# Two pads that move the weights and one input tile of a fused attention and MoE kernel by 128 and 288 bytes

## The chip, the cores and the metric

The kernel runs on one core of a Trainium2 chip. The metric is the device time of one execution in microseconds (us), the median over several executions. Lower is better.

## What is computed

Attention with mixed heads (a 12 by 12 matrix before the softmax, another after it), whose output is the input of a bilinear MoE block without gates:

```python
batch, n_heads, seq, head_dim = (4, 12, 448, 64)
n_tokens, d_model, d_ff = (1792, 768, 1536)

def _attn_ref(q, k, v, w_pre, w_post):
    scores = scale * np.matmul(q, k.transpose(0, 1, 3, 2))
    scores = np.einsum('bhij,hg->bgij', scores, w_pre)
    attn = softmax(scores)                      # max, exp, sum, divide
    attn = np.einsum('bhij,hg->bgij', attn, w_post)
    return np.matmul(attn, v).astype(np.float32)

def _moe_ref(x, w_a, w_b, w_out):               # x: the attention output, 1792 x 768
    a = x @ w_a
    b = x @ w_b
    return (a * b @ w_out).astype(np.float32)
```

## The kernel before

One program runs on all five engines, in an order that is written out by hand. It has two stages.

The attention stage takes 92 steps of up to 20 queries each: scores (`qk`, L241), head mixing (`premix`, L305), softmax (`smax`), a second mixing (`postmix`, L348) and the product with v (`av`, L384). Its output goes to DRAM, per batch b, as `xd[b]`.

The MoE stage works on four blocks of 448 tokens (b = 0 to 3). It first goes over f = 0 to 11 (128 columns of d_ff each) and b: `run_a` and `run_b` each make one 128x448 result in PSUM, from 6 slices of the contraction of 768. Then the output part goes over b and m (6 blocks of 128 output rows): `run_o` makes one 128x448 result from 12 slices of the contraction of 1536. Every product is taken in three matmuls, since both operands are split into a high and a low part: `mm3` (L545 to L547) multiplies high by high, high by low and low by high. So `run_a` and `run_b` are 18 matmuls each, `run_o` is 36, and the MoE has 12 x 4 x 36 + 24 x 36 = 2592 of them, all of one shape: 128x128 weights (the stationary operand: `wh` and `wl`) and 448 moving columns (`xhl` in the first part, `hh` and `hl` in the output part), 4 bytes per element. Each matmul has its own weight load. TensorE loads the weights of the next matmul while the present one runs.

The tiles lie in SBUF where the pools put them, one pool behind the other. What matters here is the byte address in a partition at which a tile begins, modulo 256. A moving slice has 448 x 4 = 1,792 = 7 x 256 bytes and a weight slice 128 x 4 = 512 = 2 x 256 bytes, so all slices of a tile have the tile's own value:

| tile | begins at byte | modulo 256 |
|---|---|---|
| x of b = 0, b = 1, b = 3 | 39,040; 17,536; 60,544 | 128 |
| x of b = 2 (pool `mx`) | 200,288 | 96 |
| all h (`hh`, `hl`) | 17,536; 39,040; 60,544; 83,584 | 128 |
| all weights (pool `mw`: `wh`, `wl`) | 175,712; 181,856; 188,000; 194,144 | 96 |

The text calls **lead** the address of the weights less that of the moving operand, modulo 256. It is 96 - 128 = 224 for b = 0, 1 and 3 and for all of the output part, and 0 for b = 2.

The pool `mc` holds the four buffers in which weights are converted. The pools of k, q and one tile of the scores (`short`) come behind it, and are closed when the MoE's pools `mw` and `mx` take their place (`open_moe`). x of b = 0, 1 and 3 and h stand in the pool `big`, in buffers of the attention stage, ahead of `mc`.

Of the kernel before, what the change touches and what calls it, by code (L numbers as in the profile page):

```python
# [7 lines left out]
F32 = mybir.dt.float32  # L8
# [13 lines left out]
def talking_heads_bilinear_kernel(  # L22
# [39 lines left out]
    OWN = 3  # L62
    SPREAD = 2
    RAW_AT = (73, 77)
    scale = 1.0 / float(D) ** 0.5

    chunks = []
# [26 lines left out]
    x_p = ctx.enter_context(tc.tile_pool(name="x", bufs=2))  # L94
    ps = ctx.enter_context(tc.tile_pool(name="ps", bufs=2, space=PSUM))
    mc = ctx.enter_context(tc.tile_pool(name="mc", bufs=1))
    short = ExitStack()
    k_p = short.enter_context(tc.tile_pool(name="k", bufs=10))
    q_p = short.enter_context(tc.tile_pool(name="q", bufs=4))
# [349 lines left out]
    mo, xt, wt, raws = {}, {}, {}, {}  # L449

    def open_moe():
        short.close()
        mo["w"] = ctx.enter_context(tc.tile_pool(name="mw", bufs=2))
        mo["x"] = ctx.enter_context(tc.tile_pool(name="mx", bufs=1))

    def load_x(b, parts=range(KD)):
        if b not in xt:
            pool, tag = ((big, "s"), (big, "s"), (mo.get("x"), "x"), (big, "pt"))[b]
            xt[b] = pool.tile([128, 2, KD, S], F32R, tag=tag, name="xhl")
        for i in parts:  # L460
            nc.sync.dma_start(out=xt[b].bitcast(F32)[:, 1, i], in_=xd[b][:, i])
# [14 lines left out]
    def load_raw(u, parts=1):  # L476
        kind, i, e = u
        t = raw_space().bitcast(I32).rearrange("p (c t) -> p c t", t=2)
        to, src = t.rearrange("p (k f) t -> p k (f t)", k=KD), (w_ab if kind == "f" else w_out)[i, e].bitcast(I32)
        n = KD // parts  # L480
        raws[u] = t
        return [
            lambda k=k: nc.sync.dma_start(out=to[:, k:k + n], in_=src[:, k:k + n]) for k in range(0, KD, n)
        ]
# [129 lines left out]
    def plan_moe():  # L614
# [5 lines left out]
        def load(n, fns):  # L620
            for i, fn in enumerate(fns):
                todo_at.setdefault(n + i, []).append(fn)
# [10 lines left out]

        todo_at.setdefault(RAW_AT[0], []).append(lambda: load(RAW_AT[0] + 1, load_raw(order[0], 3)))
        todo_at.setdefault(RAW_AT[1], []).append(lambda: load(RAW_AT[1] + 1, load_raw(order[1], 3)))
        s0 = last_prep + 1
# [16 lines left out]
    with tc.manual_schedule():  # L653
# [37 lines left out]
        for s in range(NU + 2):  # L691
            now[0] = s
            if s == last_prep + 1:
                open_moe()
# [164 lines left out]
```

## Time and profile before

| | |
|---|---|
| median of 3 runs | 918.71 us (914.97 to 920.8) |
| the profiled execution | 918.93 us |
| its span, from the first to the last instruction | 917.2 us |
| TensorE (PE) busy | 885.6 us (97%) |
| VectorE (DVE), ScalarE (ACT), GpSimd (POOL) busy | 515.8, 376.2, 440.2 us |

A row of the profile names a line of the program, an engine, an operation and its tiles. PE is TensorE's matmuls, PEld its weight loads, which run beside them. The duration shown for a matmul is longer than its share of the engine, since consecutive matmuls overlap: what a matmul costs is the time from its start to the start of the next one, called the **pitch** here. The view in order of time gives starts to 0.01 us, so a pitch is best read over many matmuls: the distance of two starts by the number of matmuls between them.

### The profile page before, as it was taken

The page shows a single profiled execution, that of the slowest core. Times are in us where ns is not written, and L with a number is a line of the kernel's source. Part 1 is how long each engine was busy: PE and PEld are TensorE (multiplying, and loading weights), DVE is VectorE, ACT ScalarE, POOL GpSimd, SP SyncE. Part 2 cuts the span into 40 slices and gives each one's busy share as a digit, 9 for nine tenths or more (in the row PEclk, how much of TensorE's full clock was granted, in tenths as well). Part 3 has the DMA queues.
Part 4 walks back from the last instruction along what each step waited for, and adds up shares of the span by engine and source line. Part 5 has one row for each costly group of instructions (what it writes and reads, how often), then busy time and mean ns, then how long its engine had stood idle before and what let it go on. Part 6 is the DMA issues. An engine that isn't in the chain of part 4 may idle for free.

```text
span 917.2 us, 27078 instructions
## 1 busy us (share of the span) xinstructions
PE 885.6 (97%) x11440; PEld 704.7 (77%) x11440; DVE 515.8 (56%) x907; ACT 376.2 (41%) x848; POOL 440.2 (48%) x547
## 2 busy tenths in 40 slices
PE   8899999999999898899999999999999999999998
PEld 4456565565656555799999999999999989999997
DVE  5667776576766676667654575556653545151500
ACT  5667677577666565421111111111111334343421
POOL 4687777576767663124423342324322255455552
PEclk9999999999999999999999999999999999999999
DMA  5798777568656775714533333334331664646441
GB/s 163 190 220 187 191 199 190 134 184 209 171 155 184 194 188 146 244 66 143 173 116 116 116 134 120 127 121 142 133 118 48 237 253 134 254 134 258 141 139 57
DMA packets 81850, 147.45 MB, mean 161 GB/s; under 512 B 41758, under 2 KB 61322, under 8 KB 80706
## 3 DMA queue, kind: packets, MB, share of 16 engines
q1 hardware_dynamic: 53602, 108.05, 36.7%
q0 software_dynamic: 28128, 37.68, 16.1%
q8 instruction: 90, 1.47, 0.7%
q14 instruction: 30, 0.25, 0.1%
HBM read 80.23 MB, written 26.74 MB: 117 GB/s over the span
## 4 chain that ended last, share of the span: by engine, by line
PE 89%; DMA 2%; issue 2%; DVE 2%; SPq 2%; ACT 1%; POOL 1%; ACTq 0%; DVEq 0%; POOLq 0%
PE xp L384 9%; PE pp L348 9%; PE pst L241 7%; PE mp L305 7%; PE pa L545 6%; PE pa L546 6%; PE pa L547 6%; PE po L546 6%; PE po L547 6%; PE po L545 6%; PE pb L545 6%; PE pb L546 6%; PE pb L547 6%; DMA sb<-s 2%; SPq L285 1%
## 5 line engine op out<-in xcount | busy, mean ns | idle before, releaser
L285 POOL DMA_DIRECT2D sb<-s x350 | 201.3, 584 | 93.9 <-PE mp L305 52.2
L504 POOL TENSOR_TENSOR cvm<-cvm,cvr 128x768 int32<-128x768 int32 x36 | 66.3, 1843 | 205.5 <-DVE cvm L503 205.5
L535 POOL TENSOR_TENSOR wl<-v,wh 128x768 fp32r<-128x768 f32 x48 | 93.6, 1974 | 106.7 <-ACT wh L534 106.7
L315 DVE TENSOR_REDUCE nm<-mp 124x1 f32<-124x448 f32 x180 | 104.4, 619 | 67.2 <-PE mp L305 66.8
L318 ACT ACTIVATE a<-mp,nm 124x448 f32<-124x448 f32 x180 | 112.6, 630 | 60.7 <-DVE nm L315 60.7
L384 PEld LDWEIGHTS xp<-pt,v 120*64 120x64 f32 x1536 | 76.9, 140 | 68.6 <-issue 48.0
L557 ACT COPY sa<-pa 128x448 f32<-128x448 f32 x48 | 25.6, 533 | 241.3 <-PE pa L547 241.3
L348 PE MATMUL pp<-kr,a 60*56 60x60 f32 x5760 | 103.4, 216 | 10.3 <-issue 9.4
L363 ACT COPY pt<-pp 120x480 f32<-120x480 f32 x176 | 91.1, 574 | 49.7 <-PE pp L348 49.6
L348 PEld LDWEIGHTS pp<-kr,a 60*56 60x56 f32 x5760 | 89.1, 127 | 28.4 <-issue 15.8
L567 DVE TENSOR_TENSOR hf<-pb,sa 128x448 f32<-128x448 f32 x47 | 29.4, 625 | 144.4 <-PE pb L547 107.0
L305 PE MATMUL mp<-sb,wp 60*64 60x448 f32 x720 | 100.7, 550 | 7.3 <-DMA sb<-s 3.4
L546 PE MATMUL po<-hl,wh 128*128 128x448 f32 x288 | 106.4, 369 | 0.5 <-DVE hl L582 0.5
L545 PE MATMUL po<-hh,wh 128*128 128x448 f32 x288 | 106.3, 369 | 0.0
L547 PE MATMUL po<-hh,wl 128*128 128x448 f32 x288 | 106.3, 369 | 0.0
L545 PE MATMUL pa<-xhl,wh 128*128 128x448 f32 x288 | 105.9, 368 | 0.0
L547 PE MATMUL pa<-xhl,wl 128*128 128x448 f32 x288 | 105.9, 368 | 0.0
L546 PE MATMUL pa<-xhl,wh 128*128 128x448 f32 x288 | 105.9, 368 | 0.0
L545 PE MATMUL pb<-xhl,wh 128*128 128x448 f32 x282 | 103.8, 368 | 0.0
L546 PE MATMUL pb<-xhl,wh 128*128 128x448 f32 x282 | 103.8, 368 | 0.0
L547 PE MATMUL pb<-xhl,wl 128*128 128x448 f32 x282 | 103.8, 368 | 0.0
L582 DVE TENSOR_TENSOR hl<-hl,hh 128x448 fp32r<-128x448 f32 x48 | 57.6, 1254 | 79.6 <-ACT hh L581 79.6
(75 smaller groups left out, 1375.0 us busy)
## 6 DMA issues: line engine op xcount, KB each, us to landing
sb<-s POOLq DMA_DIRECT2D x346, 105.0 KB, 4.6
v<-wod SPq DMA_DIRECT2D x24, 768.0 KB
v<-in_w_ab_dram SPq DMA_DIRECT2D x22, 768.0 KB
hd<-hf SPq DMA_DIRECT2D x48, 224.0 KB
v<-in_w_out_dram SPq DMA_DIRECT2D x12, 768.0 KB
k<-in_k_dram SPq DMA_DIRECT2D x24, 224.0 KB
v<-in_v_dram SPq DMA_DIRECT2D x48, 112.0 KB
xhl<-xd SPq DMA_DIRECT2D x24, 224.0 KB
```

What stands on the lines that cost most here:

```text
L285: (nc.sync if u <= AH and i % 2 else nc.gpsimd).dma_start(out=sbt[u][i % 2][r:r + m * H], in_=rows)
L305: nc.tensor.matmul(mt[u, i // 2][col:col + M], lhsT=wp[r:r + m, :M], rhs=tiles[i % 2][r:r + m])
L315: nc.vector.tensor_reduce(nm[:m], mp[:m], axis=AXX, op=ALU.max, negate=True)
L318: nc.scalar.activation(a[:m], mp[:m], ACTF.Exp, bias=nm[:m], scale=1.0, accum_out=rss[u][:m, j:j + 1])
L348: nc.tensor.matmul(pp_t[i][64 * e:64 * e + C, H * r:H * r + H, j, :m], lhsT=a[rows, keys:keys + C], rhs=kr[rows, j, :, :m],)
L363: nc.scalar.copy(to[:C2, :, o + QB * i:o + QB * i + QB], pp_t[i][:C2].rearrange("p x j t -> p x (j t)"))
L384: nc.tensor.matmul(xp[64 * e:64 * e + 64, p % 3, :n], lhsT=vt[b % 2][g][:C2, h % G, r], rhs=ptt[a][:C2, r, h, :n], start=(r == 0), stop=(r ...
L504: lambda: nc.gpsimd.tensor_tensor(m, m, r, op=ALU.add),
L535: nc.gpsimd.tensor_tensor(ll[:, sl], raw, hh.bitcast(F32)[:, sl], op=ALU.subtract)
L545: nc.tensor.matmul(o, lhsT=hh[:, k0 + kk], rhs=mh[:, kk], start=(kk == 0), stop=False)
L546: nc.tensor.matmul(o, lhsT=hh[:, k0 + kk], rhs=ml[:, kk], start=False, stop=False)
L547: nc.tensor.matmul(o, lhsT=ll[:, k0 + kk], rhs=mh[:, kk], start=False, stop=(kk == n - 1))
```

## The change

Two tiles that nothing reads or writes are added. The first, of 32 x 4 = 128 bytes in a partition, is in the pool `mc`, so that everything behind it begins 128 bytes later. The second, of 40 x 4 = 160 bytes, stands ahead of the x of b = 2 in the pool `mx`, which so begins 288 bytes later.

```diff
@@ -62,6 +62,8 @@
     RAW_AT = (73, 77)
+    PAD_W = 32
+    PAD_X = 40
@@ -94,6 +96,7 @@
     mc = ctx.enter_context(tc.tile_pool(name="mc", bufs=1))
+    mc.tile([128, PAD_W], F32, tag="pad", name="pad")
     short = ExitStack()
@@ -452,6 +455,7 @@
         mo["x"] = ctx.enter_context(tc.tile_pool(name="mx", bufs=1))
+        mo["x"].tile([128, PAD_X], F32, tag="pad", name="pad")
```

| tile | begins at byte, after | modulo 256 |
|---|---|---|
| x of b = 0, 1, 3 and all h | as before | 128 |
| x of b = 2 | 200,576 | 128 |
| all weights | 175,840; 181,984; 188,128; 194,272 | 224 |
| conversion buffers `cvm`, `cvr` | 128 bytes later | 224, before 96 |
| k, q, the third tile of the scores | 128 bytes later | each by 128 |

The lead is 224 - 128 = 96 everywhere. Every engine has the same instructions in the same order, with the same waits, in both kernels; only addresses differ. In the attention stage k and q move together, and both operands of L305, L348 and L384 stay where they were.

## Rows read from the trace of the kernel before

**Rows 1.** The page: engines' busy time, and granted clock by slice of the span.

```profile
PE 885.6 (97%) x11440; PEld 704.7 (77%) x11440; DVE 515.8 (56%) x907; ACT 376.2 (41%) x848; POOL 440.2 (48%) x547
PEclk9999999999999999999999999999999999999999
```

**Rows 2.** The page: the chain that ended last, by engine.

```profile
PE 89%; DMA 2%; issue 2%; DVE 2%; SPq 2%; ACT 1%; POOL 1%; ACTq 0%; DVEq 0%; POOLq 0%
```

**Rows 3.** By stretch: engines' busy us (instructions), clock, DMA share, GB/s.

```profile
0.00:379.10 379.10, 351.69 (x8849) 217.60 (x8849) 254.55 (x588) 252.93 (x598) 241.33 (x443) 0.98 0.71 183
379.10:734.00 354.90, 354.90 (x1730) 324.90 (x1729) 207.03 (x276) 56.56 (x96) 109.23 (x58) 1.00 0.38 132
734.00:913.40 179.40, 178.88 (x865) 162.18 (x863) 54.20 (x43) 66.02 (x151) 89.64 (x46) 1.00 0.50 174
```

**Rows 4.** In order of time (start us, duration us): f=0, b=0 and 1.

```profile
382.80 0.36 PE L545 MATMUL pst<-xhl,wh 128*128 128x448 f32 x1
...
393.60 0.37 PE L545 MATMUL pa<-xhl,wh 128*128 128x448 f32 x1
```

**Rows 5.** In order of time: f=1, first matmuls of b=0, 2 and 3.

```profile
408.34 0.37 PE L545 MATMUL pa<-xhl,wh 128*128 128x448 f32 x1
...
423.22 0.36 PE L545 MATMUL pa<-xhl,wh 128*128 128x448 f32 x1
...
430.52 0.36 PE L545 MATMUL pa<-xhl,wh 128*128 128x448 f32 x1
```

**Rows 6.** In order of time: two first matmuls and the last of the output part.

```profile
742.24 0.37 PE L545 MATMUL po<-hh,wh 128*128 128x448 f32 x1
...
909.64 0.37 PE L545 MATMUL po<-hh,wh 128*128 128x448 f32 x1
...
913.15 0.37 PE L547 MATMUL po<-hh,wl 128*128 128x448 f32 x1
```

**Rows 7.** By line, 383.3:393.5: xcount | busy us, mean ns | idle.

```profile
L546 PE MATMUL pb<-xhl,wh 128*128 128x448 f32 x6 | 2.2, 362 | 0.0
```

**Rows 8.** By line, 423.4:430.4, b=2.

```profile
L546 PE MATMUL pb<-xhl,wh 128*128 128x448 f32 x6 | 2.2, 365 | 0.0
```

**Rows 9.** By line, 431.4:452.6, b=3, 0 and 1: matmuls and weight loads.

```profile
L546 PE MATMUL pb<-xhl,wh 128*128 128x448 f32 x18 | 6.6, 369 | 0.0
...
L546 PEld LDWEIGHTS pb<-xhl,wh 128*128 128x128 f32 x18 | 3.4, 188 | 0.3
```

**Rows 10.** By line, 383.3:393.5: weight loads.

```profile
L547 PEld LDWEIGHTS pb<-xhl,wl 128*128 128x128 f32 x6 | 1.1, 188 | 0.1
```

**Rows 11.** Warm-up matmuls at full clock: in order of time, and by line.

```profile
15.63 1.51 PE L145 MATMUL warm<-ones 128*128 128x128 f16 x24
...
L145 PE MATMUL warm<-ones 128*128 128x128 f16 x24 | 1.5, 220 | 0.0
```

**Rows 12.** Waits, 379 to 917.2 (waiter <- releaser: us in total, times, longest).

```profile
ACT sa L557 <- PE pa L547: 241.3, 48, 8.3
POOL cvm L504 <- DVE cvm L503: 203.5, 34, 16.5
ACT so L593 <- PE po L547: 113.2, 24, 6.8
DVE hf L567 <- PE pb L547: 107.0, 34, 6.8
PEld po L546 <- DVE hl L582: 0.9, 1, 0.9
PE po L546 <- DVE hl L582: 0.5, 1, 0.5
```

**Rows 13.** The chain that ended last, around the output part's start.

```profile
731.49 2.34 ACT hh L581 x5
734.81 5.01 DVE hl L582 x3
```

## The prediction

> **What bounds the kernel now.** I read the page's first two parts, the chain, then the stretches, and last single matmuls. TensorE is busy for 885.6 of 917.2 us at nine tenths or more of the full clock of 2.4 GHz in all slices [rows 1], and holds 89% of the chain that ended last [rows 2]. The chip thus waits for TensorE alone. Up to 379.1 us it works on attention, whose matmuls keep the distance between their operands' addresses. From 379.1 to 734.0 and from 734.0 to 913.4 us it does the 1728 and 864 matmuls of the MoE and is busy for all of 354.9 and for 178.88 of 179.4 us at clock 1.00 [rows 3]. In this stage every other engine waits for TensorE: ScalarE 241.3 us for `pa` and 113.2 us for `po`, VectorE 107.0 us for `pb`; GpSimd waits for VectorE (203.5 us), and TensorE itself once, 0.5 us [rows 12]. So the MoE's time is 2592 times the pitch, and all that can change it is the pitch.
>
> **The pitch is not one number**, though shape, clock and line are the same. From the first matmul of the second group (b=0, f=0) to the first of b=2 are 54 matmuls in 393.60 - 382.80 = 10.80 us: 200.0 ns each, at lead 224 [rows 4]. In f=1, b=2 takes 36 matmuls in 430.52 - 423.22 = 7.30 us, 202.8 ns at lead 0, and b=0 and b=1 take 72 in 423.22 - 408.34 = 14.88 us, 206.7 ns at lead 224 [rows 5]. The output part runs 45 groups of 18 from 742.24 to 909.64 us: 167.40 / 810 = 206.7 ns, lead 224 [rows 6]. b=2 repeats its 202.8 and the others their 206.7 in each of the f that follow. The matmuls' own durations follow: 362, 365 and 369 ns [rows 7, 8, 9], while the weight load takes 188 ns at either end of the scale [rows 9, 10]. What stretches is the stream of the 448 columns, not the load beside it.
>
> How much there is to take: the last 24 warm-up matmuls of 128 columns, with weight loads too, take 1.51 us, the last of them 220 ns [rows 11], so their pitch is (1510 - 220) / 23 = 56.1 ns. 128 columns at 2.4 GHz are 53.3 ns, which leaves 2.8 ns of fixed cost; 448 columns would be 186.7 + 2.8 = 189.5 ns. The MoE's matmuls stand 10.5, 13.3 and 17.2 ns above that.
>
> The sum of now: 72 matmuls (f=0, b=0 and 1) at 200.0, 12 x 36 = 432 of b=2 at 202.8, and the other 2088 at 206.7 (exactly 14.88/72) make 14.4 + 87.6 + 431.5 = 533.5 us. The trace has 913.15 - 379.09 = 534.1 us from first to last start, the 0.5 us wait among it, so the sum closes.
>
> **The change part by part.** It adds no instruction, wait or DMA; only addresses differ. Three edits:
>
> *Weights 128 bytes later.* The lead of b=0, 1, 3 and of the output part, 2160 matmuls, goes from 224 to 96. No row of before has lead 96, so its pitch has to be bounded. Below stands 189.5 ns, from a stream that shows no stretch. Above, the worst row is 206.7 ns; since nothing says that it is the worst there is, I go one step further. The two levels seen at lead 224, 200.0 and 206.7, lie 6.7 ns apart (16 clocks of 2.4 GHz); the next such step is 213.3 ns. Between these ends I take 200.0 ns. Leads 224 and 0 are neighbours on the circle of 256 bytes, 32 apart, and both are stretched; 96 lies 96 and 128 bytes away, in a part of the circle that the trace has not seen. If the stretch comes from the two streams meeting at the same place of a pattern of 256 bytes, it should be less there; if the pattern is 128 bytes or shorter, 96 and 224 are the same place, which the trace shows at 200.0 as well as at 206.7. 200.0 is the lower row, and lies near the middle of the floor and the common level.
>
> *x of b=2 to lead 96.* Its 432 matmuls leave 202.8 ns for whatever lead 96 gives. At 200.0 this is 1.2 us of gain, at 206.7 a loss of 1.7 us.
>
> *All else that moves* (conversion buffers, k, q, one tile of scores) I cost at nothing. k and q keep their distance, L305, L348 and L384 keep both operands. The conversions are on VectorE, ScalarE and GpSimd, which are busy for 207, 57 and 109 of 355 us in the first part and 54, 66 and 90 of 179 us in the second [rows 3]; the cover is TensorE's 533 us of matmuls, and would hold at the floor of 491 us too. DMA engines are at 0.38 and 0.50 there. One place has no cover: at the start of the output part TensorE waits 0.5 us for `hl` of VectorE [rows 12], which works from 734.81 on through 5.01 us of the chain, after ScalarE's `hh` [rows 13]. VectorE's pace there doesn't change, while the two blocks of matmuls ahead of it (72) end 72 x 6.7 ns = 0.5 us sooner at 200.0; I add 0.4 us to this wait.
>
> Sum: 2592 x 200.0 = 518.4 us in place of 533.5, -15.1 us, +0.4 us. Against the profiled execution, 918.93 us (0.2 above the median of the runs, so nothing is corrected): 904.2 us, 1.6% faster.
>
> A rule of the Trainium skill speaks against this. Its page "TensorE: Matmul & The Clock Gate" (section "Step-by-step: what each phase is for") has two independent SBUF read ports in TensorE, one for moving columns and one for weights, and says that loading the next weights takes no read bandwidth from the running matmul. By that rule the lead could not matter, and the sum would be nothing. The trace disagrees: pitch and duration differ by the tile that is read, 202.8 against 206.7 ns and 365 against 369 [rows 5, 8, 9].
>
> **Rivals.**
>
> *The streams no longer meet*: 189.5 ns everywhere. For it: both known leads are close together, and 96 is far from them. Against: even the best stretch seen is 10.5 ns above the floor, and the weight load sweeps 512 bytes, twice round the circle, so it may always meet the columns somewhere. 2592 x 189.5 = 491.2 us, -42.3: 876.6 us, with the wait of `hl` 877 to 878.
>
> *The change doesn't do what it says*: the pitch hangs on lead modulo 128 or less, or on where x itself begins. Then all settles at 206.7, since 2088 of the 2160 matmuls at lead 224 do so now, and b=2 loses its advantage: 2592 x 206.7 = 535.7 us, +2.2: 921.1 us. For it: 96 and 224 are alike modulo 128, and lead 224 has two levels with nothing but their history between them. If lead 0's 202.8 held everywhere instead, 525.7 us, -7.8: 911 us.
>
> *Lead 96 is worse*: one more step, 213.3 ns in all: 552.9 us, +19.4: 938.3 us. For it: the two leads seen do not show the worst. Against: they stand where small shifts of timing carry the pitch between levels, which looks like an edge rather than a quiet region. It decides from (533.5 + 9.2) / 2592 = 209.4 ns on.
>
> **How the numbers follow.** About 200.0 ns 0.33; at or near the floor (up to 195 ns) 0.20; 202.8 everywhere 0.07; all at 206.7 0.22; worse 0.18. The likeliest is 904.2 us, its own range 900 to 908. About 1% (9.2 us) is what a measurement here can tell from no change. Faster takes the first two cases, 0.53; same those at 202.8 and 206.7, 0.29; slower 0.18. The range leaves out the last: from 875 us, just below the floor's case, to 922 us, just above the case of no effect.
>
> **What would show it.** In the profile after, the MoE's stretch is 2592 pitches: 518 us if I am right, 491 at the floor, 536 without effect, 553 if worse. The mean durations of L545 to L547 should be 362 ns in all groups, b=2 as the others; 352 (362 - 10.5) would be the floor, 369 no effect, over 372 the last rival. Weight loads should stay at 188 ns, and the attention stage at 379 us. The wait of L546 for `hl` should stay under 2 us. The forecast is wrong if the groups of one lead still differ, if b=2 now differs from the others at the same lead, or if the stretch moves while the durations of matmuls don't.

## The result: 0.8% faster in the first set of runs, 13 us in four later ones, and a profile that hit the forecast

In 22 runs of each kernel the median went from 921.31 to 915.11 us; the ratio is 0.9919, with a 95% interval of 0.9892 to 0.9946. This is faster by 0.8%, half the forecast; the medians lie 6.2 us apart, where 14.7 were forecast. Seven executions of the changed kernel, all over 917.5 us, count as slow and are left out of the ratio; with six of them in (the seventh, 1415.06 us, had a granted clock of 0.556) the gain would be 0.6%. The profiled execution of the changed kernel took 903.93 us, the fastest of its 22, where the forecast was 904.2. Both are true, and the experiments are about how.

The page after, engines and chain, as [rows 1, 2]:

```profile
PE 868.3 (96%) x11440; PEld 703.2 (78%) x11440; DVE 518.8 (57%) x907; ACT 377.5 (42%) x848; POOL 442.5 (49%) x547
PE 76%; POOL 8%; issue 6%; DMA 5%; DVE 2%; ACT 1%; SPq 1%; POOLq 0%; ACTq 0%; DVEq 0%
```

By stretch, as [rows 3] (attention, first part of the MoE, output part; the columns are the same):

```profile
0.00:378.90 378.90, 349.37 (x8849) 216.74 (x8849) 255.14 (x588) 254.03 (x598) 242.81 (x443) 0.99 0.71 183
378.90:724.60 345.70, 345.70 (x1731) 324.53 (x1730) 209.63 (x276) 56.70 (x96) 110.29 (x58) 1.00 0.39 135
724.60:898.50 173.90, 173.23 (x865) 161.89 (x863) 53.98 (x43) 66.13 (x151) 89.39 (x46) 1.00 0.51 179
```

The attention stage is as long as before, though TensorE holds less of the chain: 76% of the whole against 89%. The first part went from 354.9 to 345.7 us, the output part from 179.4 to 173.9: 14.7 us, all of it in TensorE's own stream. In order of time, f=1, the first matmuls of b=0, 2 and 3, as [rows 5]:

```profile
407.79 0.36 PE L549 MATMUL pa<-xhl,wh 128*128 128x448 f32 x1
...
422.19 0.36 PE L549 MATMUL pa<-xhl,wh 128*128 128x448 f32 x1
...
429.39 0.36 PE L549 MATMUL pa<-xhl,wh 128*128 128x448 f32 x1
```

72 matmuls in 14.40 us and 36 in 7.20: 200.0 ns for b=0, 1 and 2 alike. The groups by line over 395 to 735 us, and the output part (740 to 895 us), as [rows 7 to 9], and the wait for `hl`, as [rows 12]:

```profile
L550 PE MATMUL pb<-xhl,wh 128*128 128x448 f32 x276 | 100.0, 362 | 0.0
L550 PE MATMUL po<-hl,wh 128*128 128x448 f32 x259 | 93.9, 362 | 0.0
PE po L550 <- DVE hl L586: 0.7, 1, 0.7
```

362 ns in all groups, which is the row that the forecast named. In this execution the whole MoE runs at 200.0 ns, but for its first matmul and the wait for `hl`.

### The profile page after: what moved, and what is told of

The parts are those of the page before. It is cut to its first block, busy times and chain, and to the rows that moved or that the text cites. A ratio compares the mean times of both kernels' runs of the same rounds, so it can differ in the third digit from the quotient of the medians.

```text
span 902.2 us, 27078 instructions
## 1 busy us (share of the span) xinstructions
PE 868.3 (96%) x11440; PEld 703.2 (78%) x11440; DVE 518.8 (57%) x907; ACT 377.5 (42%) x848; POOL 442.5 (49%) x547
## 4 chain that ended last, share of the span: by engine, by line
PE 76%; POOL 8%; issue 6%; DMA 5%; DVE 2%; ACT 1%; SPq 1%; POOLq 0%; ACTq 0%; DVEq 0%
POOL sb L288 6%; PE pa L549 6%; PE pa L550 6%; PE pa L551 6%; PE po L550 6%; PE po L551 6%; PE po L549 6%; PE pb L550 6%; PE pb L549 6%; PE pb L551 6%; PE xp L387 6%; PE pp L351 5%; PE mp L308 4%; PE pst L244 4%; DMA sb<-s 2%
## 5 line engine op out<-in xcount | busy, mean ns | idle before, releaser
L351 PE MATMUL pp<-kr,a 60*56 60x60 f32 x5760 | 104.6, 216 | 13.4 <-issue 12.8
L550 PE MATMUL po<-hl,wh 128*128 128x448 f32 x288 | 104.5, 363 | 0.7 <-DVE hl L586 0.7
L549 PE MATMUL pa<-xhl,wh 128*128 128x448 f32 x288 | 104.5, 363 | 0.0
L550 PE MATMUL pa<-xhl,wh 128*128 128x448 f32 x288 | 104.4, 362 | 0.0
L551 PE MATMUL po<-hh,wl 128*128 128x448 f32 x288 | 104.4, 362 | 0.0
L549 PE MATMUL po<-hh,wh 128*128 128x448 f32 x288 | 104.4, 362 | 0.0
L549 PE MATMUL pb<-xhl,wh 128*128 128x448 f32 x282 | 102.2, 362 | 0.0
L550 PE MATMUL pb<-xhl,wh 128*128 128x448 f32 x282 | 102.2, 362 | 0.0
```

The costliest lines, as they stand in the source:

```text
L351: nc.tensor.matmul(pp_t[i][64 * e:64 * e + C, H * r:H * r + H, j, :m], lhsT=a[rows, keys:keys + C], rhs=kr[rows, j, :, :m],)
L549: nc.tensor.matmul(o, lhsT=hh[:, k0 + kk], rhs=mh[:, kk], start=(kk == 0), stop=False)
L550: nc.tensor.matmul(o, lhsT=hh[:, k0 + kk], rhs=ml[:, kk], start=False, stop=False)
L551: nc.tensor.matmul(o, lhsT=ll[:, k0 + kk], rhs=mh[:, kk], start=False, stop=(kk == n - 1))
```

## The experiments

Theory A: the lead sets the pitch, and executions differ only in the attention stage. Theory B: a lead has several **levels** of the pitch; the stream of matmuls falls to one at its start or after a disturbance (called a **draw** here), and keeps it.

**The changed kernel, unaltered, profiled again** (four calls, each on another chip).

> The changed kernel, unaltered, profiled once more. The recorded profile of it has the MoE at 200.0 ns per matmul throughout (518.4 us), and its execution of 903.93 us is the fastest of 22, whose median is 915.1; the kernel before has a median of 921.3. Theory A (the lead fixes the pitch; the spread comes from the attention stage, up to 379 us): the MoE again takes 518 to 520 us with every matmul at 200.0 ns, and what exceeds 904 us lies before the first MoE matmul. Theory B (lead 96 has two levels as well, and which one holds is a matter of timing): part of the MoE runs at 203 to 207 ns, the MoE takes 522 to 536 us, and the attention stage ends at 379 us as before.

> The changed kernel, unaltered, in more rounds beside lead 192. Theory B gives its executions four places, by the level drawn at the MoE's entry (1728 matmuls) and after the wait for hl (the last 830 or so): 904 us (200.0 and 200.0), 910 (the output part at 206.7), 915 to 916 (the first part at 206.7), 921 (both), each with the 3 us or so that the attention stage varies by. If none but the lead counted, all would be at 902 to 909 us.

> The changed kernel, unaltered, once more in five rounds. Theory B: the profiled execution has the first part and the output part each at 200.0 or at 206.7 ns; in the five profiles so far both were at 200.0. Executions at 904 to 906 us plus 0, 5.5, 11.5 or 17 us, plus what this chip's attention stage takes beyond 379 us (on one chip it was 386 us). If only the attention stage varied, the profile again shows 519 us for the MoE and the excess ahead of it.

> The changed kernel, unaltered, beside lead 192 on one chip. In six profiles so far its MoE took 519.3 us and the attention stage 379 to 386 us; the executions that other calls timed lie at 903 to 912 us for the most part, those of the first set at 904 to 920. If the first set's longer executions came from second-level draws, this set should show steps of 5.5 and 11.5 us above its shortest that lead 192 lacks. If they came from the attention stage, both kernels spread alike.

Medians, beside the kernel before on the same chip: 905.05 against 917.86, 910.04 against 923.00, 909.61 against 923.43, 910.24 against 923.20 us; ratios 0.9880 (0.9843 to 0.9917), 0.9844 (0.9797 to 0.9891), 0.9880 (0.9829 to 0.9932), 0.9872 (0.9835 to 0.9910). The difference of the medians is 12.8 to 13.8 us in each. The profiles say where the rest went. By stretch (length, then PE busy, clock, DMA share, GB/s), the second repeat:

```profile
0.00:386.42 386.42, 354.08 (x8849) 0.98 0.70 179
386.42:732.13 345.71, 345.71 (x1730) 1.00 0.39 135
732.13:905.68 173.55, 172.88 (x865) 1.00 0.51 180
```

and the fourth, with two starts of its output part, 834 matmuls apart, and a group of that part (740 to 895 us):

```profile
0.00:381.50 381.50, 350.22 (x8848) 0.98 0.70 182
381.50:727.22 345.72, 345.72 (x1731) 1.00 0.38 135
727.22:906.31 179.09, 178.42 (x864) 1.00 0.49 174
...
733.55 0.36 PE L549 MATMUL po<-hh,wh 128*128 128x448 f32 x1
...
905.90 0.37 PE L549 MATMUL po<-hh,wh 128*128 128x448 f32 x1
...
L550 PE MATMUL po<-hl,wh 128*128 128x448 f32 x251 | 92.2, 367 | 0.0
```

Both theories get something. In the second repeat the attention stage is 7.5 us longer and the MoE is not. The first and the third are alike, with attention stages of 380.0 and 383.2 us. But in the fourth, 912.08 us, nothing was altered and the output part took 179.1 in place of 173.6 us: it fell to 206.7 ns (172.35 us / 834) after the wait for `hl`, at lead 96. Theory A is wrong. The matmuls there last 367 ns; at lead 224 they last 369 at the same pitch, so a duration tells the level only within a lead.

**A nudge of 56 ns at the entry.** One or two 16-bit matmuls of 128 columns ahead of the MoE's first matmul (in `run_a`; `range(2)` in the second kernel); no address of the MoE's operands changes:

```diff
         pa = ps.tile([128, 512], F32, tag="m", name="pa", bufs=3)[:, :S]
+        if f == b == 0:
+            for _ in range(1):
+                nc.tensor.matmul(pa[:, :128], lhsT=ones, rhs=ones)
         mm3(pa, hh, ll, x[:, 0], x[:, 1], KD)
```

> The changed kernel with one 16-bit matmul of 128 columns (56 ns) ahead of the first matmul of the MoE, which only moves its time against whatever the level is drawn from; all leads stay at 96. Theory B: the first part falls to 200.0 or to 206.7 ns and stays there for its 1728 matmuls (MoE 519 or 531 us). Theory A: 200.0 ns, 519 us.

> The same with two such matmuls. Theory B: 200.0 or 206.7 ns throughout the first part, not necessarily as with one. Theory A: 200.0 ns.

By stretch, the MoE's two parts with one nudge, then with two:

```profile
387.02:744.21 357.19, 357.19 (x1732) 1.00 0.38 131
744.21:923.32 179.11, 178.59 (x864) 1.00 0.50 174
```

```profile
389.11:734.81 345.70, 345.70 (x1731) 1.00 0.39 136
734.81:913.90 179.09, 178.42 (x864) 1.00 0.50 174
```

With one, all 2592 matmuls run at 206.7 ns and the MoE takes 536.3 us; that is the second rival's MoE, reached without a change of lead. With two, the first part is at 200.0 and the output part at 206.7. So the levels of lead 96 are worth 357.2 - 345.7 = 11.5 us and 179.1 - 173.6 = 5.5 us, drawn twice in an execution. Each of the two kernels ran once. That the nudge made the draw at the entry, and not chance, is likely, since the seven profiles of this MoE without it all entered at 200.0 ns; it is not shown.

**Each part of the change alone.** First only x of b=2 is moved, so that the lead is 224 throughout (`PAD_W` left out, `PAD_X = 8`); then only the weights (`PAD_X` left out), so that b=2 is at lead 0.

> One part alone: x of b=2 is moved by 32 bytes, the weights stay, so that the lead is 224 in the whole MoE. In the kernel before, lead 224 ran at 200.0 ns in f=0 (b=0, b=1) and at 206.7 ns ever after the first passage of b=2 at lead 0; the bursts at lead 224 gave 200.0, 204.4 and 206.7 ns. Theory A (the lead alone sets the pitch, and 224 is a 206.7 lead): 206.7 ns in all of the MoE, 535.7 us, 920 to 921 us. Theory B (each lead has several levels, and the stream keeps the one that it fell into until something disturbs it): with no b=2 at another lead to disturb it, the first part stays at the level at which f=0 enters; if that is 200.0 ns, the first part takes 346 us in place of 355, and the wait for hl at the start of the output part draws again: 906 us if it draws 200.0, 912 if 206.7.

> The other part alone: the weights 128 bytes later, x of b=2 left behind them, so that b=2 is at lead 0 and all else at lead 96. b=2 (432 matmuls) should run at 202.7 or 206.7 ns. Each passage of b=2 is a disturbance: if lead 96 returned to 200.0 by itself, the MoE would take 521 us; if it keeps what it falls into, b=3, 0 and 1 run at 200.0 or 206.7 in each f, 521 to 533 us.

By stretch, x alone, then the weights alone:

```profile
377.48:734.69 357.21, 357.21 (x1731) 1.00 0.38 131
734.69:913.83 179.14, 178.61 (x865) 1.00 0.50 174
```

```profile
380.37:727.60 347.23, 347.23 (x1730) 1.00 0.38 135
727.60:906.71 179.11, 178.44 (x864) 1.00 0.49 174
```

With x alone the profiled execution (919.59 us) entered at 206.7 and stayed there; three others, not profiled, took 905.87, 912.67 and 916.24 us, which would fit such draws. The ratio of these three is 0.9889 (0.9833 to 0.9945). With the weights alone b=2 runs at 202.7 and b=3 comes back to 200.0 in each f, so the first part loses 1.5 us; here the output part drew 206.7. Ratio 0.9940 (0.9898 to 0.9982).

**All leads.** Bursts of the same matmul behind the end of the kernel, the columns' start shifted by 32 bytes at a time. Two kernels have 36 bursts of 24; the third has 127, and in it (`SEQ` lists lead, length, columns of weights and moving columns of each burst):

```diff
+        def burst(hh, x, lead, n_, wc=128, cols=S):
+            mv, ws = x.rearrange("p f s -> p (f s)"), hh.rearrange("p k f -> p (k f)")
+            i = (96 - lead) // 32 % 8
+            t = ps.tile([128, 512], F32, tag="x", name="scan", bufs=1)[:wc, :cols]
+            for n in range(n_):
+                wo, mo_ = 128 * (n % 4), S * (n % 4) + 8 * i
+                nc.tensor.matmul(t, lhsT=ws[:, wo:wo + wc], rhs=mv[:, mo_:mo_ + cols], start=(n == 0), stop=(n == n_ - 1))
...
             run_o(j)
+        for lead, n_, wc, cols in SEQ:
+            burst(last, ht[B - 1][0], lead, n_, wc, cols)
```

> The changed kernel with 36 bursts of 24 matmuls of the same shape behind its end (128x128 weights, 448 columns, results unused), whose moving operand starts 0 to 7 times 32 bytes later, so that each lead of the circle of 256 bytes is visited, once from bursts at lead 96 and once from bursts at lead 0; four bursts move weights and columns together by 32, 64 and 160 bytes. It adds about 175 us. If the pitch is set by the lead modulo 256: lead 0 near 202.8 ns, 224 near 206.7 or 200.0, 96 at 200.0, and the others a curve between 189.5 and 213 ns; moving both operands together changes nothing. If the pattern has 128 bytes or less: leads 32 and 160, 64 and 192, 96 and 224 give the same. If it hangs on where the columns themselves begin: the bursts that move both change their pitch. The MoE ahead of the scan is another sample of the changed kernel: 200.0 ns by theory A, a mixture by theory B.

> The kernel before with the same 36 bursts behind its end, at the same sequence of leads (its weights lie 128 bytes elsewhere). The pitch of each lead should be that of the other scan if the lead alone counts, and differ by burst if the absolute addresses count. The MoE ahead of it is another sample of the kernel before: 206.7 ns at b=0, 1, 3 and in the output part and 202.8 at b=2, if its recorded profile is typical.

> The changed kernel with 127 bursts behind its end: 16 matmuls at leads 96, 192, 224 and 0, each entered from bursts of 12 and of 13 matmuls at each of the seven other leads (14 entries a lead), then bursts of 24 whose weights have 128, 64 and 32 columns, then bursts with 448, 320 and 224 moving columns. Theory B: the entries at 224 and 0 split between several levels, those at 96 and 192 fall nearly all to 200.0; theory A: one level per lead. If the stretch above 189.5 ns comes from the weight load's reading beside the columns, it shrinks with the weights' columns (10.5 ns at 128, about half at 64, about a quarter at 32) and stays, in ns per matmul, as the moving columns get fewer (320 columns 146.7 + 10.5 = about 147 ns at least with fixed cost, 224 about 107); if it is a fixed cost of such a matmul, it stays at 10.5 ns for fewer weights' columns.

The two scans agree in each burst to within 0.2 ns, though their absolute addresses differ. They are two executions, so in these bursts the level follows from the stream just before and is not chance. Moving weights and columns together left lead 96 at 200.0 ns; at lead 224 it gave 204.4 and 206.7, levels that this lead has unmoved too. Two bursts at lead 96 in the scan of the changed kernel, two starts of each, 15 matmuls apart:

```profile
924.67 0.56 PE L826 MATMUL scan<-hh,wh 128*128 128x448 f32 x2
...
927.67 0.56 PE L826 MATMUL scan<-hh,wh 128*128 128x448 f32 x2
...
935.01 0.57 PE L826 MATMUL scan<-hh,wh 128*128 128x448 f32 x2
...
938.11 0.56 PE L826 MATMUL scan<-hh,wh 128*128 128x448 f32 x2
```

3.00 / 15 = 200.0 and 3.10 / 15 = 206.7 ns. The pitch, as a mean over a steady pattern that repeats after 1 to 5 matmuls, and how 14 entries per lead ended in the third kernel:

| lead | levels, ns | entries |
|---|---|---|
| 0 | 202.7, 206.7 | 10, 4 |
| 32 | 203.3, 204.4 | |
| 64 | 202.2 | |
| 96 | 200.0, 206.7 | 11, 3 |
| 128 | 204.0 | |
| 160 | 205.3 | |
| 192 | 200.0 | 14 |
| 224 | 200.0, 204.4, 206.7 | 4, 4, 6 |

No lead goes below 200.0. Bursts with fewer columns of weights, then with fewer moving columns, all at lead 96, two starts of each, 15 matmuls apart:

```profile
1292.08 0.56 PE L751 MATMUL scan<-hh,wh 128*32 128x448 f32 x2
...
1295.08 0.57 PE L751 MATMUL scan<-hh,wh 128*32 128x448 f32 x2
...
1317.22 0.60 PE L751 MATMUL scan<-hh,wh 128*128 128x320 f32 x3
...
1319.42 0.60 PE L751 MATMUL scan<-hh,wh 128*128 128x320 f32 x3
...
1324.70 0.50 PE L751 MATMUL scan<-hh,wh 128*128 128x224 f32 x3
...
1326.38 0.49 PE L751 MATMUL scan<-hh,wh 128*128 128x224 f32 x3
```

A quarter of the weights leaves the pitch as it was: at lead 96 it is 200.0 ns with 32 columns as with 128, and 201.6 with 64. At lead 0 it goes from 202.7 to 202.2, at lead 128 from 204.0 to 202.2. So the stretch is not in proportion to what the weight load reads. With 320 moving columns the pitch is 146.7 ns, 13.3 above 320 / 2.4, as 200.0 is above 448 / 2.4; with 224 it is 111.7 (1675 ns / 15, before the starts are rounded), 18.3 above. So these 4-byte matmuls stood 13.3 ns or more above their columns' time at each of the three sizes, where I took 2.8 from the 16-bit warm-up, and no one constant fits all three. The expectation named 147 ns for 320 columns, but its sum is wrong (320 / 2.4 is 133.3, not 146.7), so that the match is luck.

**Disturbing the stream.** The changed kernel with 12 to 15 matmuls at another lead ahead of each f from 1 on and of each output block (`burst(wt["f", f][0], xt[0][:, 0], KICK[f % 7], 12 + f % 2)` ahead of `run_a(f, 0)`, and so ahead of `run_o`).

> The changed kernel with 12 or 13 matmuls at another lead ahead of each f from 1 on, and of 12 to 15 ahead of each block of the output part (other leads in turn, results unused); some 90 us more. Each is followed by 144 (first part) or 36 (output part) matmuls at lead 96 without a break. Theory A: all that follow run at 200.0 ns, but for a few at the border. Theory B: after some of the disturbances the matmuls at lead 96 run at 206.7 ns, as one of eleven bursts did, and stay there through the 144 or 36 until the next disturbance. If they come back to 200.0 by themselves, lead 96 draws the stream back, and lead 224 differs from it in that.

Of 35 stretches 16 ran at 206.7 ns to their end. In order of time, the first matmul after the disturbance at f=5 and the first of the next one, 144 matmuls later:

```profile
533.40 0.36 PE L550 MATMUL pa<-xhl,wh 128*128 128x448 f32 x1
...
563.16 0.37 PE L751 MATMUL scan<-xhl,wh 128*128 128x448 f32 x1
```

29.76 us / 144 = 206.7 ns: once lead 96 is at its upper level, it does not come back by itself.

**Lead 192 in the whole MoE** (`PAD_W = 56`, `PAD_X = 16`), alone, with the nudge, and with 35 disturbances (lead 96 in place of 192 among them; the expectation's 19 of 35 for lead 96 is a miscount of 16).

> The change with other sizes of the pads: weights 224 bytes later, x of b=2 also at 128, so that the lead is 192 in the whole MoE. Both bursts at lead 192 ran at 200.0 ns (198, 201, 201 in turn). Theory A: as the changed kernel, 519 us for the MoE, 903 to 909 us. Theory B: the same, unless lead 192 has a second level that the two bursts didn't meet; then some stretch of the MoE runs above 200 ns.

> Lead 192 in the whole MoE, beside the changed kernel on the same chip. All 16 entries into lead 192 in the bursts ended at 200.0 ns on the mean, while 4 of 26 at lead 96 ended at 206.7. Theory B: all executions at 902 to 909 us, and a median below the changed kernel's by what that draws at 206.7 (0 to 11 us). Theory A: no difference from the changed kernel.

> Lead 192 on the same chip. Its level was 200.0 ns after all of 35 disturbances and 16 entries, so it should spread by the attention stage alone. Equal medians if the changed kernel draws 200.0 in nearly all executions; 2 us or more below it otherwise.

> Lead 192 with the one 16-bit matmul ahead of the MoE that threw the changed kernel to 206.7 ns for all of its MoE (536.3 us). If lead 192 has one level on the mean, the MoE stays at 200.0 ns and 519 us; if its level is drawn like that of lead 96, some part of it is above.

> Lead 192 with the 35 disturbances of the earlier kernel (12 to 15 matmuls at another lead ahead of each f from 1 on and of each block of the output part). At lead 96 these left 19 of 35 stretches at 206.7 ns. If lead 192 has one level, all 35 return to 200.0 ns within a dozen matmuls; if it has several, some stay above.

All 35 stretches come back to 200.0 ns. The one at f=5 takes 28.81 us for 144:

```profile
537.29 0.37 PE L550 MATMUL pa<-xhl,wh 128*128 128x448 f32 x1
...
566.10 0.37 PE L751 MATMUL scan<-xhl,wh 128*128 128x448 f32 x1
```

By stretch, with the nudge:

```profile
384.96:730.66 345.70, 345.70 (x1732) 1.00 0.38 135
730.66:904.26 173.60, 172.89 (x865) 1.00 0.51 180
```

Against the kernel before its ratios are 0.9836 (0.9791 to 0.9880), 0.9857 (0.9814 to 0.9899) and 0.9827 (0.9781 to 0.9873). Beside the changed kernel on one chip its median is 904.87 against 910.24 us in one set, 909.86 against 910.04 in another. It is the better of the two in what it is thrown to, and no worse in either set. In the first of these sets its executions took 904.3 to 905.7 us, but for one of 912.4, and those of the changed kernel spread from 905.7 to 921.6, without clear steps. Draws of lead 96 would do that; of the two profiles there, the changed kernel's has 5.5 us more in the output part and 2.3 in the attention stage.

## Why the prediction was half right

*What bounds, and what moves*: right for the MoE. All of the profile's gain is pitch, the weight load still overlaps, other engines kept up. The attention stage took 378.9 us in this profile, near the 379 named; over all profiles it took 376.4 to 389.1, so a single execution could not be forecast to 1 us. The wait for `hl` grew by 0.2 us (0.5 to 0.7), where I had added 0.4.

*The value of 200.0 ns*: right for the profiled execution, and the sum with it: 14.7 us forecast, 14.7 in the profile. The reason for it was not right. I argued that the stretch should be less, far from leads 0 and 224; lead 128 is as far from them as lead 96 and ran at 204.0 ns, above the 202.8 of lead 0. That lead 96 has a level at 200.0 was luck.

*The step that failed* is the multiplication 2592 x 200.0 as if a lead had one pitch. I had the contrary in hand: the prediction says that lead 224 shows two levels "with nothing but their history between them", and then gives lead 96 only one. Lead 96 has 206.7 as well, drawn once at the entry (11.5 us) and once after the wait for `hl` (5.5 us). The forecast should have been a mixture of 904, 909.7, 915.7 and 921 us. Whether the kernel before also draws after that wait is not shown: in both its profiles its output part is at 206.7 ns.

*How much of the first set that explains* stays open. Its executions of the changed kernel lie at 904 to 920 us for the most part, but only one was profiled. Of the seven profiles of this MoE unaltered (the five of this kernel and the two with bursts behind its end) six have both parts at 200.0. The attention stage adds up to 7.5 us in them, and not by chip alone: on one chip it took 382.5 to 389.1 us in four profiles of different kernels. For draws speaks that 15 of the first set's 22 executions took from 912.4 to 930.4 us, where lead 192 took at most 912.4 in 15 of its 16. Against draws as the whole cause speaks a count: of ten profiles (those seven, the two with a nudge, and the weights alone) four have the output part and one the first part at 206.7. At these rates draws would cost 0.4 x 5.5 + 0.1 x 11.5 = 3.4 us on the mean, an estimate; the first set lacks 14.7 - 6.2 = 8.5. The four later sets, with 13 us, are near the forecast.

*The rivals.* The floor of 189.5 ns is refuted: no lead, and no smaller weight load that was tried, went below 200.0. I had carried a fixed cost over from a 16-bit matmul to a 4-byte one. The MoE without effect, 536 us, exists at lead 96 as a pair of draws, seen once, with the nudge; a mean pitch of 213.3 ns was not seen at any lead.

*The rule of the Trainium skill* ("TensorE: Matmul & The Clock Gate", "Step-by-step: what each phase is for") was that loading weights takes no read bandwidth from the running matmul. The runs leave this much of it: at lead 96 the pitch is the same with a quarter of the weights, which speaks against lost bandwidth there; at lead 128 it fell by 1.8 ns. That operand addresses therefore don't matter does not follow: at one shape and clock the mean pitch goes from 200.0 to 206.7 ns with them and with the draw. What in the chip makes the levels was not found.

## What to carry to other kernels

Where TensorE is the bound, read the distance between matmul starts for each operand tile apart; where equal shapes have unequal pitch, as here, look at where the tiles begin in a partition, and try a pad, which costs a few bytes of SBUF. Before trusting a pitch, disturb the stream by one short matmul and look again: of two offsets that profile alike, take the one that comes back (here weights 192 bytes ahead, not 96). A single profile shows one draw; where the median of many runs lies above it by steps, look for the same work at another level.

## What the runs showed of the hardware

- A stream of 128x448 matmuls on 4-byte data settled into a pattern of 1 to 5 matmuls whose mean pitch is one of a few levels from 200.0 to 206.7 ns, at full clock. The lead modulo 256 bytes decides which levels were seen; 64 and 192 differ (202.2 and 200.0 ns), so the pattern is longer than 128 bytes.
- A level held for 1728 matmuls where nothing disturbed it. After 12 to 15 matmuls at another lead, lead 96 went on at 206.7 ns in 16 of 35 cases and lead 192 in none; a single matmul of 56 ns ahead was probably enough to choose the level, once.
- Such a matmul stood 13.3 ns above its columns at 2.4 GHz at best (200.0 ns for 448 columns, 146.7 for 320), and 18.3 ns for 224 columns (111.7).
- The same attention stage took 376.4 to 389.1 us, and differed by up to 6.6 us on one chip.
